# The last 512 rows of w_down on partitions 0 to 63, loaded in two pieces of 32 partitions

## The chip, the cores and the metric

The kernel runs on one core of one Trainium2 chip. The metric is the device time of one execution in microseconds (us). "The span" is what the profile shows, from the first to the last instruction; the time is about 2 us longer than the span. Before the change the median is 123.2 us.

## The reference, cut to what matters

```python
x  = A_x                                   # [8, 1, 512]
xn = layernorm(x)
s  = attention(xn, k_cache, v_cache, wq, wo)   # last 1024 keys, 32 heads on 8 kv heads
g  = silu((gelu(xn @ w_gate) * (xn @ w_up)) @ w_down)   # 512 -> 1792 -> 512
return x + s * g
```

Eight rows of activations meet 47.5 MB of weights and cache, each byte used once. So the kernel is a stream of loads with a little work behind it. In the order of loading: K, wq, then K and V in turn, w_gate, w_up, w_down (1792 rows of 512 numbers in bf16, 1 KB a row), and wo in four blocks of 1 MB.

## The kernel before

All loads of weights and cache go out from SyncE's queue, each a DMA of 128 partitions:

```python
    def load_ffn():
        ...                                    # w_gate, w_up: two loads of 896 KB each
        JH = JF // 2                           # JF = 14 rows of w_down per partition
        wd = B_w_down.rearrange("(p j) d -> p j d", j=JF)
        for a in range(2):
            t = slot()[:, 0 : JH * D].rearrange("p (j d) -> p j d", j=JH)
            nc.sync.dma_start(out=t, in_=wd[:, a * JH : (a + 1) * JH, :])
            wd_t.extend(t[:, j, :] for j in range(JH))
    ...
    def load_wo(m, cut=HS):                    # HS = 8; the last block in two pieces, 6 + 2
        t = slot().rearrange("p (e d) -> p e d", e=HS)
        src = A_wo[m * HS * Dh : (m + 1) * HS * Dh, :].rearrange("(p e) d -> p e d", e=HS)
        for lo, hi in ((0, cut), (cut, HS)):
            if lo < hi:
                nc.sync.dma_start(out=t[:, lo:hi, :], in_=src[:, lo:hi, :])
        wo_t[m] = t
```

The up and down projections run on TensorE in four groups of 32 columns (NQ = 4, Q = 32):

```python
    def ffn_up():                              # 2 x 4 x 4 matmuls of 512 columns
        ...
                cols = wt[k // 2][:, k % 2, :].rearrange("x (p j) -> x j p", j=JF)
                for q in range(NQ):
                    nc.tensor.matmul(gu_ps[w][Q * q : Q * (q + 1), :], xpT_sb[:, k, :],
                                     cols[:, j0[q] : j0[q] + JQ, :], ...)
    def ffn_down():                            # 14 x 4 matmuls
        ...
    # at the end: four output stores, two from SyncE's queue, two from ScalarE's
    for q in range(NQ):
        eng = nc.sync if q % 2 == 0 else nc.scalar
        eng.dma_start(out=out_flat[:, q * P : (q + 1) * P], in_=out_sb[32 * q : 32 * q + B, :])
```

The softmax here doesn't subtract the row's maximum and nothing guards it: scores larger than these inputs give would overflow.

## Time and profile before

| | before |
|---|---|
| time, median | 123.2 us |
| span | 121.1 us |
| chain of waits, share of DMA | 82% |
| 768 KB piece of the last A_wo block landed | 116.70 us |
| end of out_sb (last arithmetic) to end of span | 2.7 us |
| 16 KB packets of the instruction queue | 14 |

From the profile page of the kernel before: the span; then, in forty slices, the busy tenths of the sixteen DMA engines and their rate; then the instruction queue (packets, MB, share of time).

```profile
span 121.1 us, 4123 instructions
...
DMA  3999999999999999999999999999999999999820
GB/s 84 387 430 430 430 427 417 419 430 425 425 427 427 425 414 422 430 419 430 425 427 422 422 417 430 422 425 422 425 433 418 422 414 434 416 430 423 341 88 5
...
q8 instruction: 14, 0.23, 0.7%
```

The loads run at about 425 GB/s from the second slice to the 37th; the fall to 341 in slice 38 is the first sign that not all sixteen engines end together. The end of the chain of waits (start, length in us, what):

```profile
98.97 17.74 DMA slot<-in_A_wo_dram
116.70 0.04 issue
116.75 1.05 PE s_ps L383 x31
117.80 0.02 issue
117.82 0.30 DVE tmp L483
118.12 0.02 issue
118.14 0.29 DVE out_sb L485
```

A piece of A_wo lands, 1.05 us of matmuls follow, two VectorE steps, and the stores. From the timeline of the same kernel, the four blocks of that last projection (start, length, engine, line; in brackets the idle time before it and what ended it):

```profile
109.96 1.02 PE L383 MATMUL s_ps<-slot,oE_1066 128*8 128x128 bf16 x32 [0.32 <-DMA slot<-in_A_wo_dram]
112.40 1.02 PE L383 MATMUL s_ps<-slot,oE_1569 128*8 128x128 bf16 x32 [1.42 <-DMA slot<-in_A_wo_dram]
114.84 1.02 PE L383 MATMUL s_ps<-slot,oE_2072 128*8 128x128 bf16 x32 [1.42 <-DMA slot<-in_A_wo_dram]
116.75 1.02 PE L383 MATMUL s_ps<-slot,oE_2360 128*8 128x128 bf16 x32 [0.88 <-DMA slot<-in_A_wo_dram]
```

TensorE waits for every block. Work that is added ahead of it is free as long as it fits into these waits; work added to the loads is not.

One more reading is needed, which no view prints. A DMA of 128 partitions is sixteen shares, and each share raises the DMA's semaphore when it lands. The trace has these raises. Sorted, in us from the span's start, for the two pieces of the last A_wo block:

```
768 KB: 113.54 113.55 113.57 113.58 113.77 113.85 114.14 114.42 114.97 115.00 116.42 116.50 116.53 116.65 116.67 116.70
256 KB: 114.17 114.18 114.20 114.22 114.41 114.48 114.78 115.06 115.61 115.64 117.06 117.12 117.15 117.27 117.31 117.32
```

Sixteen equal shares end over 3.2 us. At 20 us they had lain within 0.3 us. The lag comes in steps of about 1.2 us, one beside each of the fourteen 16 KB packets of the instruction queue: by 74 us, after eight packets, eight engines are late by one step; the next six packets hit six of these a second time. These packets are refills of TensorE's instructions: it has 3714 instructions (1856 matmuls, 1856 weight loads and two semaphore waits), 14.5 times 256, and 256 instructions of 64 bytes make 16 KB. (That one is 64 bytes is this arithmetic.) A second instruction queue has 8 KB packets; the two that run beside loads (41.45 and 79.19 us) leave a smaller step, of 0.6 to 0.9 us, in one share each. A DMA is done when its last share is, so the kernel waits for the engines that carried most refills.

### The profile page before, as it was taken

To read this page: it belongs to the slowest core of one execution; us is meant where nothing else is said; L and a number is where in the kernel's file an instruction comes from. 1 tells how busy PE (TensorE), PEld (TensorE's weight loads), DVE (VectorE), ACT (ScalarE), POOL (GpSimd) and SP (SyncE) were. 2 spreads that over 40 slices of the span, in tenths; PEclk is the share of its full clock that TensorE was granted. 3 is DMA by queue.
4 is the path that set the end of the run, shared out by engine and by line. 5 is a ranking of instruction groups with operands and counts; after the bars stand their busy time and mean duration, and the time that the engine had idled before them with its cause. 6 is when DMAs were issued, how large, how long until landed. Compare 5 with 4: busy or idle time off the path is not lost.

```text
span 121.1 us, 4123 instructions
## 1 busy us (share of the span) xinstructions
PE 86.0 (71%) x1856; PEld 71.1 (59%) x1856; DVE 72.3 (60%) x150; ACT 22.6 (19%) x70; POOL 2.4 (2%) x15
## 2 busy tenths in 40 slices
PE   0075269696875968999997969566798789955450
PEld 0061029586865957999896969565698542134340
DVE  2352046866956749678989987747798670562000
ACT  0440000321303301212330330303033300300000
POOL 6100000000000000000000000000000000000000
PEclk9999756999999985559999999999999756995555
DMA  3999999999999999999999999999999999999820
GB/s 84 387 430 430 430 427 417 419 430 425 425 427 427 425 414 422 430 419 430 425 427 422 422 417 430 422 425 422 425 433 418 422 414 434 416 430 423 341 88 5
DMA packets 6929, 47.73 MB, mean 394 GB/s; under 512 B 888, under 2 KB 896, under 8 KB 1920
## 3 DMA queue, kind: packets, MB, share of 16 engines
q1 hardware_dynamic: 6800, 47.46, 93.7%
q8 instruction: 14, 0.23, 0.7%
q10 hardware_dynamic: 112, 0.02, 0.1%
q14 instruction: 3, 0.02, 0.1%
HBM read 47.46 MB, written 0.01 MB: 392 GB/s over the span
## 4 chain that ended last, share of the span: by engine, by line
DMA 82%; PE 12%; DVE 2%; SPq 1%; issue 0%
DMA slot<-in_A_k_cache_dram 44%; DMA slot<-in_B_w_gate_dram 16%; DMA slot<-in_A_wo_dram 15%; DMA slot<-in_A_wq_dram 7%; PE kT_ps L282 7%; PE m_ps L329 2%; PE sc_ps L294 2%; SPq L91 1%; PE s_ps L383 1%; DVE kT L286 1%; PE m_ps L316 1%; DVE sums L318 1%; SPq L103 0%; PE m_ps L370 0%; DVE tmp L483 0%
## 5 line engine op out<-in xcount | busy, mean ns | idle before, releaser
L286 DVE COPY kT<-kT_ps 128x1024 bf16<-128x1024 bf16 x64 | 42.2, 677 | 18.1 <-PE kT_ps L282 17.5
L282 PE MATMUL kT_ps<-ident,slot 128*128 128x128 bf16 x512 | 43.4, 234 | 9.9 <-DMA slot<-in_A_k_cache_dram 9.5
L282 PEld LDWEIGHTS <-slot 128*128 128x128 bf16 x512 | 32.6, 104 | 13.3 <-DMA slot<-in_A_k_cache_dram 10.1
L304 ACT ACTIVATE pT<-sc_ps,diag 128x128 bf16<-128x128 f32 x64 | 18.2, 368 | 70.6 <-PE sc_ps L294 70.6
L294 PE MATMUL sc_ps<-qT_all,kT 128*128 128x16 bf16 x512 | 22.9, 171 | 0.3 <-issue 0.3
L329 PE MATMUL m_ps<-pT,slot 128*128 128x16 bf16 x512 | 21.8, 170 | 1.2 <-issue 1.1
L329 PEld LDWEIGHTS <-slot 128*128 128x128 bf16 x512 | 18.6, 97 | 4.6 <-issue 3.1
L294 PEld LDWEIGHTS <-kT 128*128 128x128 bf16 x512 | 20.4, 99 | 0.0
L318 DVE TENSOR_REDUCE sums<-m_ps 128x16 f32<-128x512 f32 x16 | 10.9, 684 | 1.2 <-PE m_ps L316 1.2
L402 PE MATMUL m_ps<-slot,xpT_sb 128*32 128x512 bf16 x32 | 7.7, 1105 | 0.0
L316 PE MATMUL m_ps<-pT,ones_pp 128*128 128x512 bf16 x16 | 6.7, 416 | 0.7 <-ACT pT L304 0.7
L250 PE MATMUL m_ps<-slot,xnT_sb 128*32 128x512 bf16 x32 | 3.5, 527 | 4.2 <-DMA slot<-in_A_wq_dram 4.2
L234 PE MATMUL m_ps<-ident,xhat 8*128 8x8 bf16 x4 | 0.3, 168 | 7.0 <-DVE xhat L214 7.0
L259 DVE CAST q_sb<-m_ps 128x512 bf16<-128x512 f32 x2 | 1.3, 686 | 6.6 <-PE m_ps L250 6.6
L356 DVE TENSOR_TENSOR wide<-m_ps,hmask 64x1024 bf16<-64x1024 bf16 x4 | 4.9, 1216 | 0.5 <-PE m_ps L352 0.4
L483 DVE TENSOR_TENSOR tmp<-s_ps,g_sb 128x128 f32<-128x128 f32 x1 | 0.3, 292 | 7.1 <-PE s_ps L383 7.1
L250 PEld LDWEIGHTS <-xnT_sb 128*32 128x32 bf16 x32 | 0.8, 101 | 6.2 <-issue 5.8
L322 DVE RECIPROCAL recip<-sums 128x16 f32<-128x16 f32 x16 | 4.0, 253 | 0.6
L234 PEld LDWEIGHTS <-xhat 8*128 8x128 bf16 x4 | 0.2, 102 | 7.0 <-DVE xhat L214 7.0
L402 PEld LDWEIGHTS <-xpT_sb 128*32 128x32 bf16 x32 | 1.7, 117 | 4.3 <-issue 3.4
L338 DVE TENSOR_TENSOR oT_all<-m_ps,recip 128x16 bf16<-128x16 f32 x16 | 3.5, 218 | 0.4 <-PE m_ps L329 0.3
L352 PE MATMUL m_ps<-ident,oT_all 128*64 128x128 bf16 x4 | 1.0, 253 | 2.7 <-DVE sums L318 2.1
(71 smaller groups left out, 33.4 us busy)
## 6 DMA issues: line engine op xcount, KB each, us to landing
slot<-in_A_k_cache_dram SPq DMA_DIRECT2D x16, 1024.0 KB, 19.4
slot<-in_A_v_cache_dram SPq DMA_DIRECT2D x16, 1024.0 KB, 19.7
slot<-in_A_wq_dram SPq DMA_DIRECT2D x4, 1024.0 KB, 8.6
slot<-in_A_wo_dram SPq DMA_DIRECT2D x3, 1024.0 KB, 18.0
slot<-in_B_w_gate_dram SPq DMA_DIRECT2D x2, 896.0 KB, 20.0
slot<-in_B_w_up_dram SPq DMA_DIRECT2D x2, 896.0 KB, 18.9
slot<-in_B_w_down_dram SPq DMA_DIRECT2D x2, 896.0 KB
slot<-in_A_wo_dram SPq DMA_DIRECT2D x1, 768.0 KB, 17.7
```

The source lines that it names most:

```text
L250: nc.tensor.matmul(q_ps[n][Q * q : Q * (q + 1), :], xnT_sb[:, k, :], wq_t[k][:, hkv * NW : (hkv + 1) * NW], start=(k == 0), stop=(k == NDC ...
L282: nc.tensor.transpose(t_ps[:, c * P : (c + 1) * P], k_t[g][:, cc * Dh : (cc + 1) * Dh], ident)
L286: nc.vector.tensor_copy(out=kT[n], in_=t_ps)
L294: nc.tensor.matmul(sc[g][:, s * CB + c, :], kT[n][:, c * P : (c + 1) * P], qT_all[:, hkv, b0 : b0 + I, :], start=True, stop=True,)
L304: nc.scalar.activation(out=pT[g][:, :, i * rep : (i + 1) * rep], in_=sc[g][:, :, i * rep : (i + 1) * rep], func=ACT.Exp, bias=diag[:, i : ...
L316: nc.tensor.matmul(sums_ps, ones_pp, pT[g], start=True, stop=True)
L318: nc.vector.tensor_reduce(out=sums, in_=sums_ps.rearrange("p c m -> p m c"), axis=AX.X, op=ALU.add)
L322: nc.vector.reciprocal(out=recip[g], in_=sums)
L329: nc.tensor.matmul(oT[g], v_t[g][:, c * Dh : (c + 1) * Dh], pT[g][:, c, :], start=(c == 0), stop=(c == C - 1),)
L338: nc.vector.tensor_tensor(out=oT_all[:, hkv * rep : (hkv + 1) * rep, b0 : b0 + I].rearrange("p j i -> p i j"), in0=oT[g].rearrange("p (i j ...
L356: nc.vector.tensor_tensor(out=wide, in0=t_ps.rearrange("p (q e) -> p e q", e=HS) .unsqueeze(2) .to_broadcast([HS * B, HS, HS, DQ]), in1=hm ...
L402: nc.tensor.matmul(gu_ps[w][Q * q : Q * (q + 1), :], xpT_sb[:, k, :], cols[:, j0[q] : j0[q] + JQ, :], start=(k == 0), stop=(k == NDC - 1), ...
```

## The change

The intent: w_down need not be spread evenly. Its last 512 rows go to partitions 0 to 63 as eight rows each, in two pieces of 32 partitions. The DRAM side of each piece is written with an outer dimension of 8, so that the piece is cut in eight shares of four partitions, on DMA engines 0 to 7 (by the rule that the prediction cites; experiment e1 looks at it). These then carry 144 KB of w_down each, the others 80 KB, where all carried 112 KB. If the engines that are late are 8 to 15, this evens them out. The price is more and smaller instructions on TensorE, since the hidden dimension is now split 10 x 128 + 8 x 64. The code calls the rows on 128 partitions wide and those on 64 narrow.

```diff
-        JH = JF // 2
-        wd = B_w_down.rearrange("(p j) d -> p j d", j=JF)
+        JH = JW // 2                                   # JW = 10, F1 = 1280
+        wd = B_w_down[0:F1, :].rearrange("(p j) d -> p j d", j=JW)
         for a in range(2):
             ...
+        t = slot()[0:PN, 0 : JN * D]                   # PN = 64, JN = 8
+        wn = B_w_down[F1:F, :].rearrange("(y x j) d -> x y (j d)", x=NX, j=JN)
+        for h in range(2):
+            nc.sync.dma_start(out=t[32 * h : 32 * (h + 1), :], in_=wn[8 * h : 8 * (h + 1)])
+        wd_t.extend(t[:, j * D : (j + 1) * D] for j in range(JN))
 ...
-                for q in range(NQ):                    # up: one matmul of 512 columns
-                    nc.tensor.matmul(gu_ps[w][Q * q : Q * (q + 1), :], xpT_sb[:, k, :],
-                                     cols[:, j0[q] : j0[q] + JQ, :], ...)
+                for q in range(NQ):                    # up: one wide, one narrow, 448 columns
+                    for first, d, c in ((True, dst[:, 0:nw], wide_c[:, w0:w1, :]),
+                                        (False, dst[:, nw:FQ], narrow_c[:, n0:n1])):
+                        nc.tensor.matmul(d, xpT_sb[:, k, :], c, ...)
 ...
-        for c in range(JQ):                            # 4 transposes, 1 copy
+        for c in range(3): ...                         # 3 transposes of 128, 3 of 64, 2 copies
 ...
-        for j in range(JF):                            # down: 14 x 4 matmuls
+        for j in range(JW + JN):                       # down: 18 x 4, the last 8 x 4 with 64 rows
```

## The prediction

> **What bounds the kernel now.** The loads. The chain of waits is 82% DMA, and the slice table shows the sixteen DMA engines 90% or more busy at about 425 GB/s from slice 2 to slice 36. Its tail: the first piece (768 KB) of the last block of A_wo is landed at 116.70 us, then 32 matmuls of L383 (1.02 us), then two DVE steps and the output store. All other work ends in time: PE waits 1.4 us before each of the A_wo blocks 1 and 2 and 0.9 us before the last (timeline).
>
> **The loads are unequal.** The trace's semaphore records give the landing of each of a DMA's sixteen shares. At 20 us they lie within 0.3 us. For the 768 KB piece, eight shares land at 113.54 to 114.42 us, two at 114.97 and 115.00, six at 116.42 to 116.70. The last piece (256 KB): eight at 114.17 to 115.06, eight at 115.61 to 117.32. Between, steps of about 1.2 us appear, each beside one of the fourteen 16 KB packets of the instruction queue (22.5 to 113.7 us). The first eight packets delay eight different engines once, later ones six of these again. The Trainium skill (Runtime: NRT & Kernel Launch, "Instruction fetch mechanics") says that instructions are refilled in 16 KiB blocks by DMA; the trace agrees on the size. The records do not number the engines. Chaining packets by end and next start, the delayed engines of the first fetches are mostly ones that did not carry the 8-row x loads. The Trainium skill (DMA: Bandwidth & Descriptors, "Why a DMA increments its semaphore by 16 and not by 1") says a DMA of this kind uses the largest k up to 16 that divides the slowest dimension of both sides, on the lowest-numbered k engines. So x used engines 0 to 7, and the late half should be 8 to 15.
>
> **The change.** By the same rule each new piece (source outer dimension 8, destination 32) goes to engines 0 to 7. Of w_down an engine now moves 112 KB. After, engines 8 to 15 move 80 KB and 0 to 7 move 144 KB. An 8192-byte packet takes 306 ns from start to start, a 7168-byte one 268, a 6144-byte one 231; estimate for 5120 bytes 193. Late engines: 16 x 268 to 16 x 193, minus 1.2 us. Early engines: plus 8 x 306 minus 1.2, plus 1.25 us. The 768 KB piece then lands on the early half at 114.8 to 115.7, on the late half by 115.5; the last piece at 116.3. The tail starts 1.0 us earlier.
>
> **Added work, off the path.** 50 more matmuls with their weight loads: L402 grows from 32 to 64 shorter ones (448 columns per group instead of 512, narrow ones with a worse stride), the down projection from 56 to 72, transposes from 4 to 6; one more copy. Estimate: plus 0.5 to 2 us before A_wo's projection, which has over 2 us of slack. The extra instructions may bring one more fetch; it would fall on an engine delayed once only, so cost nothing. Two more DMAs and one more ring slot: issues run some 17 us ahead, no stall.
>
> **Prediction.** 122.2 us (minus 0.8%), 121.8 to 122.8. Faster by over 2%: 0.02; within 2%: 0.96; slower: 0.02.
>
> **What would show it.** The sixteen last shares land within about 2 us instead of 3.1, the last at 116.3; the wait of L383 for A_wo ends near 115.7; its 1.02 us is unchanged; span near 120.1.
>
> **What would make it wrong.** If the late half is 0 to 7: about 124.4. If the pieces spread over sixteen engines: no gain. If the narrow strided matmuls cost over 3 us more, PE becomes the end of the chain.

## The result, and the profile after

The changed kernel takes 125.11 us (median of 4 runs, 124.96 to 125.12) against 123.22 us: a ratio of 1.015, with a 95% interval of 1.0132 to 1.0167. It is 1.5% slower, clear of the noise though under 2%, where a gain of 0.8% was predicted; the measured time lies far outside the predicted range of 121.8 to 122.8 us.

From the page of the changed kernel:

```profile
span 123.4 us, 4227 instructions
...
DMA  3999999999999999999999999999999999999400
GB/s 72 406 420 433 425 425 428 428 430 425 422 425 420 422 417 425 420 428 420 433 420 425 425 430 425 422 420 425 425 418 430 417 425 421 429 428 393 164 5 5
...
q8 instruction: 14, 0.23, 0.7%
```

The full rate does not last longer, and the slack at the end has changed shape: one slice at 164 GB/s, where there had been one at 341. One engine seems to run on alone. The chain of waits ends so:

```profile
103.35 14.46 DMA slot<-in_A_wo_dram
117.81 0.04 issue
117.85 1.05 PE s_ps L399 x26
118.90 0.02 issue
118.92 0.30 DVE tmp L514
119.22 0.02 issue
119.25 0.29 DVE out_sb L516
```

The 768 KB piece lands at 117.81 us, 1.11 us later than before, where 115.7 was predicted. From there to the end of out_sb it is 1.73 us in both. The four blocks in the timeline:

```profile
109.67 1.03 PE L399 MATMUL s_ps<-slot,oE 128*8 128x128 bf16 x32
112.02 1.03 PE L399 MATMUL s_ps<-slot,oE 128*8 128x128 bf16 x32 [1.32 <-DMA slot<-in_A_wo_dram]
116.02 1.02 PE L399 MATMUL s_ps<-slot,oE 128*8 128x128 bf16 x32 [2.97 <-DMA slot<-in_A_wo_dram]
117.85 1.02 PE L399 MATMUL s_ps<-slot,oE 128*8 128x128 bf16 x32 [0.81 <-DMA slot<-in_A_wo_dram]
```

The first starts earlier than before, although TensorE had more to do before it, and the second too, by 0.4 us. Then the third block comes 4.0 us after the second instead of 2.44. The loss falls into one interval, between 112 and 116 us. The shares, from the semaphore records:

```
second block: 108.17 108.48 109.59 110.49 110.56 110.60 110.66 110.99 111.02 111.08 111.10 111.19 111.20 111.45 111.97 111.98
third block:  110.62 110.92 112.03 112.99 113.07 113.08 113.11 113.43 113.47 113.58 113.59 113.62 113.64 113.90 114.42 115.97
768 KB:       112.44 112.74 113.92 114.80 114.87 114.89 114.95 115.33 115.36 115.38 115.44 115.48 115.53 115.73 116.29 117.81
```

The plan has worked on fourteen engines: eleven of them are now within 1 us of each other, three are ahead. One of the two that were last at 111.98 needs 4.0 us for its 64 KB of the third block instead of 2.45, and is alone at the end by 1.5 us. The fourteenth 16 KB packet starts at 111.94 us. So it seems that the last engine was loaded by the change and then struck by a refill; if so, it is not one that the change relieved. Experiment e11 tests this.

The second loss is at the very end: from the end of out_sb (119.54) to the end of the span (123.4) it takes 3.9 us, before it took 2.7. SyncE's waits after 118 us, changed kernel (who waited for whom: us in total, times, longest):

```profile
SPq L519 <- DVE out_sb L516: 13.7, 1, 13.7
SPq L547 <- DMA out_dram<-out_sb: 1.6, 1, 1.6
```

and the kernel before:

```profile
SPq L488 <- DVE out_sb L485: 13.1, 1, 13.1
SPq L516 <- DMA out_dram<-out_sb: 0.7, 3, 0.4
```

One wait of 1.6 us for a store stands where there had been three short ones. The stores of the two kernels in the timeline, before and then changed (start, length, queue, count):

```profile
118.47 0.71 SPq L488 DMA_DIRECT2D out_dram<-out_sb  x2
118.47 0.65 ACTq L488 DMA_DIRECT2D out_dram<-out_sb  x2
```

```profile
119.56 1.07 SPq L519 DMA_DIRECT2D out_dram<-out_sb  x2
119.57 0.65 ACTq L519 DMA_DIRECT2D out_dram<-out_sb  x2
```

ScalarE's two stores go out in 0.65 us as before; SyncE's take 1.07 instead of 0.71. In the trace SyncE pauses 0.45 us before its second store, and the store's last share lands at 122.33 us, 0.74 us after its other shares; between, at 121.01 us, an 8 KB packet of the second instruction queue starts. So the longer end has three parts: the last store starts 0.37 us later after out_sb than before (the pause), takes 0.57 us longer to land (its one late share), and 0.22 us more pass from its landing to the end of the span. The last part goes with the order in which SyncE waits for the semaphores at the end, which e12 looks at.

In sum: +1.1 us by the loads and +1.2 us at the end make the span 2.3 us longer. The time rose by 1.9 us only. The part of the time outside the span was 2.1 us for the kernel before and 1.7 to 1.9 us for the changed one in the four runs; nothing in the profile explains that part, and it stays open.

### The profile page after: what moved, and what is told of

It reads as the page before. It is cut to its first block, busy times and chain, and to the rows that moved or that the text cites. A ratio compares the mean times of both kernels' runs of the same rounds, so it can differ in the third digit from the quotient of the medians.

```text
span 123.4 us, 4227 instructions
## 1 busy us (share of the span) xinstructions
PE 85.5 (69%) x1906; PEld 72.5 (59%) x1906; DVE 71.7 (58%) x151; ACT 22.5 (18%) x70; POOL 2.4 (2%) x15
## 4 chain that ended last, share of the span: by engine, by line
DMA 93%; SPq 2%; PE 1%; DVE 0%; issue 0%
DMA slot<-in_A_k_cache_dram 59%; DMA slot<-in_B_w_up_dram 15%; DMA slot<-in_A_wo_dram 12%; DMA slot<-in_A_wq_dram 7%; SPq L101 1%; PE s_ps L399 1%; SPq L113 0%; DVE tmp L514 0%; DVE out_sb L516 0%; SPq L149 0%; SPq L120 0%
## 5 line engine op out<-in xcount | busy, mean ns | idle before, releaser
L298 PE MATMUL kT_ps<-ident,slot 128*128 128x128 bf16 x512 | 42.6, 231 | 11.7 <-DMA slot<-in_A_k_cache_dram 11.3
L298 PEld LDWEIGHTS <-slot 128*128 128x128 bf16 x512 | 32.0, 103 | 15.6 <-DMA slot<-in_A_k_cache_dram 12.4
L345 PEld LDWEIGHTS <-slot 128*128 128x128 bf16 x512 | 18.4, 96 | 3.1 <-issue 1.3
L399 PE MATMUL s_ps<-slot,oE 128*8 128x128 bf16 x128 | 4.1, 306 | 5.1 <-DMA slot<-in_A_wo_dram 5.1
L424 PE MATMUL m_ps<-slot,xpT_sb 128*32 128x384 bf16 (+3 forms) x64 | 6.8, 589 | 0.0
L266 PE MATMUL m_ps<-slot,xnT_sb 128*32 128x512 bf16 x32 | 4.2, 618 | 3.7 <-DMA slot<-in_A_wq_dram 3.7
L399 PEld LDWEIGHTS <-oE 128*8 128x8 bf16 x128 | 3.2, 116 | 5.9 <-issue 5.9
L332 PE MATMUL m_ps<-pT,ones_pp 128*128 128x512 bf16 x16 | 6.0, 376 | 0.7 <-ACT pT L320 0.7
L424 PEld LDWEIGHTS <-xpT_sb 128*32 128x32 bf16 x64 | 3.3, 119 | 2.7 <-issue 2.5
```

The costliest lines, as they stand in the source:

```text
L266: nc.tensor.matmul(q_ps[n][Q * q : Q * (q + 1), :], xnT_sb[:, k, :], wq_t[k][:, hkv * NW : (hkv + 1) * NW], start=(k == 0), stop=(k == NDC ...
L298: nc.tensor.transpose(t_ps[:, c * P : (c + 1) * P], k_t[g][:, cc * Dh : (cc + 1) * Dh], ident)
L332: nc.tensor.matmul(sums_ps, ones_pp, pT[g], start=True, stop=True)
L345: nc.tensor.matmul(oT[g], v_t[g][:, c * Dh : (c + 1) * Dh], pT[g][:, c, :], start=(c == 0), stop=(c == C - 1),)
L399: nc.tensor.matmul(s_ps[32 * q : 32 * q + B, :], oE[m][:, e, :], wo_t[m][:, e, q * P : (q + 1) * P], start=(m == 0 and e == 0), stop=(m == ...
L424: nc.tensor.matmul(d, xpT_sb[:, k, :], c, start=(k == 0 and first), stop=(k == NDC - 1), skip_group_check=True,)
```

## The experiments

Theory A: the late engines are not 8 to 15; some are in 0 to 7, and the one struck by the fourteenth refill has got the extra load. Theory T: the end is longer because of SyncE's own instructions. Rivals: the added work of TensorE, the added DMAs as such, and the extra load on engines 0 to 7 alone, without refills.

### e1_map: which engine is late

```diff
+    def mark(k):                       # 128 bytes to each of k partitions: k shares
+        nc.sync.dma_start(out=mark_sb[0:k, k * 64 : (k + 1) * 64],
+                          in_=A_wq[0:k, k * 64 : (k + 1) * 64])
 # kernel before, with mark(15) ... mark(1) one by one behind the later big loads
```

> The kernel before with fifteen tiny marker loads of 1 to 15 partitions (128 bytes each) between the last big loads; results stay right. The landing of a marker of k partitions gives the lag of DMA engines 0 to k-1, so the markers number the engines. The step that I relied on (late half = engines 8 to 15) expects every engine of the 8-partition marker to be among the eight early ones (lag under 0.9 us), and all of 8 to 15 late by 1.2 us or more. Theory A (read off the landings of the changed kernel) expects six of the late eight above 7 and two of them in 0 to 7, and that one of these two is struck by the fourteenth instruction refill. Time as before within 0.5 us.

The run is a single one (state unknown, 123.64 us, 768 KB piece at 116.70 us, as in the kernel before). The landings of the markers of 9 to 5 partitions (k shares each; each marker also has one early raise by the sequencer itself, left out):

```
9: 89.23 89.27 89.33 89.34 89.43 89.90 90.13 90.69 90.73
8: 91.78 91.83 91.84 91.96 92.44 92.66 93.15 93.19
7: 93.92 93.95 94.08 94.52 94.75 95.32 95.37
6: 96.09 96.13 96.24 96.68 96.92 97.54
5: 98.26 98.31 98.40 98.82 99.09
```

Each marker is a list of lags of engines 0 to k-1. From 9 to 8 an early engine drops out: engine 8 is early. From 8 to 7 again: engine 7 is early. From 7 to 6 one of the two late ones goes, from 6 to 5 the other: engines 6 and 5 are late. Engines 0 to 4 are early. The markers of more partitions place engines 9, 10 and 11 among the late, and leave one early engine in 12 to 15 that they don't number. So the assumption that the late half is 8 to 15 is wrong in two places of eight, and theory A's first half is shown.

The page "DMA: Bandwidth & Descriptors" of the Trainium skill, section "Why a DMA increments its semaphore by 16 and not by 1", says that such a DMA uses the largest k up to 16 that divides the slowest dimension of both sides, on the lowest-numbered k engines. The trace agrees with the count: a marker of k partitions had k landings for each k from 1 to 13 that was read, and each 32-partition piece had 8. That they are the lowest-numbered engines is the page's word; the nesting of the lists above fits it.

### e11_map_after: which engine ends last in the changed kernel

```diff
 # changed kernel
         load_wo(m, cut=HS if m < NM - 1 else HS - 2)
+        if m == 2:
+            for k in (5, 6, 7, 8):
+                mark(k)
```

> The changed kernel with four marker loads of 5, 6, 7 and 8 partitions between the third and the last block of A_wo: their landings give the lags of engines 0 to 4, 0 to 5, 0 to 6 and 0 to 7 just there. Theory A expects that engine 5 or engine 6 is the one that lands last of all sixteen (1.5 us after the next) since the fourteenth refill struck it, so the marker of 5 partitions lands some 2 us before the third block's last share and the marker of 7 after it. If the last engine is above 7, all four markers land 1.5 us or more before it.

A single run (state unknown). The last share of the third block landed at 115.91 us, then came:

```
5: 113.22 113.33 113.81 113.90 114.13
6: 113.46 113.54 113.99 114.10 114.33 116.12
7: 113.72 113.76 114.17 114.30 114.52 114.60 116.33
```

The sixth engine, engine 5, is the last of all; engine 6 is next but one step better. Theory A's second half is shown: the change put 32 KB more on engine 5, and beside the fourteenth refill (112.18 us in this run) the same engine fell back by 1.5 us. One run shows which engine it is; that one share lands alone, 1.5 us after the rest and at 117.7 to 117.8 us, is the same in the traces of the changed kernel, e5 and e9. The time was 124.23 us, 0.9 us less than the changed kernel without markers, though the 768 KB piece landed at 117.77 us; the four more loads are SyncE's, and the end shrank from 3.9 to 3.0 us. That belongs to theory T below.

### e7_fewer: take the fourteenth refill away

```diff
     def transpose_block(n):            # changed kernel, wrong result on purpose
         g, s = n // NB, n % NB
+        if s == NB - 1:
+            kT[n] = kT[n - 1]
+            return
```

> The changed kernel, wrong results on purpose: the last of each group's four blocks of K is not transposed, the block before is used again. That takes 256 instructions from TensorE (3814 to 3558), one refill's worth, all else equal. Theory A (the fourteenth refill, at 111.9 us, strikes engine 5 or 6, which the change loaded more) expects thirteen refills before the loads end, the 768 KB piece of A_wo at about 116.3 us instead of 117.8, and about 123.6 us in all, the longer end kept. Rival (added load on engines 0 to 7 alone sets the end, refills or not): the piece stays near 117.8.

The last block of K in each group is replaced by the one before it, so the result is wrong on purpose, though the comparison with the reference still let it pass. The ratio to before was 1.0073 (1.001 to 1.0137; 123.65, 123.65, 123.75 and one 125.09 us, whose span was as short as the others'). Thirteen 16 KB packets came before the loads ended. The chain of waits:

```profile
103.24 13.09 DMA slot<-in_A_wo_dram
116.37 1.05 PE s_ps L402 x32
```

The 768 KB piece landed at 116.33 us, where theory A had 116.3 and the rival 117.8. The extra load on engines 0 to 7 is in this kernel in full, so by itself it costs nothing here (116.33 against 116.70 us before); with the refill on top it costs 1.5 us. The end is still 3.7 us long.

### e2_sixteen and e3_half: two controls that were none

```diff
-        for h in range(2):             # e2: same rows, same partitions, sixteen shares
-            nc.sync.dma_start(out=t[32 * h : 32 * (h + 1), :], in_=wn[8 * h : 8 * (h + 1)])
+        HC = JN * D // 2
+        for h in range(2):
+            nc.sync.dma_start(out=t[:, HC * h : HC * (h + 1)], in_=wn[:, :, HC * h : HC * (h + 1)])
```

> The changed kernel with its 64-partition piece of w_down loaded as two column halves of 64 partitions, source outer dimension 16: shares of four partitions on all sixteen engines. Everything else, TensorE work included, stays as changed. Theory A (the extra 1.25 us of load on an engine in 0 to 7 that is struck twice by refills) expects the 768 KB piece of A_wo to land about as before, near 116.7 us instead of 117.8. Rival B (the added instructions of TensorE, with the fourteenth refill at 111.9 instead of 113.7 us) expects it to stay near 117.8. The end of the program after out_sb took 2.7 us before and 3.9 us changed: if that goes with the engine assignment, the time is 123.2; if with the added instructions or loads, 124.3.

It ran 127.46 us, ratio 1.0354 (1.0314 to 1.0393): slower than everything else, which no theory had expected. The rate in stretches of 2 us (stretch, length, busy time of the engines, clock, DMA share, GB/s), e2_sixteen:

```profile
104.00:106.00 2.00, 1.57 (x16) 0.46 (x8) 1.22 (x4) 0.58 (x1) 0.00 (x0) 1.00 1.06 245
106.00:108.00 2.00, 0.91 (x14) 0.63 (x14) 1.25 (x5) 0.00 (x0) 0.00 (x0) 1.00 0.98 210
108.00:110.00 2.00, 0.92 (x48) 0.80 (x52) 0.15 (x1) 0.00 (x0) 0.00 (x0) 0.82 1.10 248
```

and the changed kernel in the first two of these:

```profile
104.00:106.00 2.00, 1.38 (x16) 0.47 (x8) 1.37 (x3) 0.46 (x1) 0.00 (x0) 1.00 1.06 445
106.00:108.00 2.00, 0.94 (x18) 0.66 (x22) 1.17 (x5) 0.00 (x0) 0.00 (x0) 1.00 0.99 418
```

While the narrow piece loads, all sixteen engines are as busy and move half as much. The page "SBUF — State Buffer" of the Trainium skill, section "Door 1: The DMA port swizzle", gives a reason: partitions 32 apart share one of sixteen ports, so partitions 0 to 63 reach eight ports only. Sixteen shares of four partitions put two engines on every port; the eight shares of the change put one. The trace agrees, with 210 to 248 GB/s instead of 418 to 445; no run here tells the port from another cause of the halved rate. So e2 is no test of theory A, and says that the eight-share form was the right way to fill 64 partitions.

> Half the dose: of the 64-partition piece, columns of the first half go to all sixteen engines, those of the second half in two pieces to engines 0 to 7. Theory A expects the latest landing half way between e2_sixteen and the changed kernel (about 117.2 us for the 768 KB piece), since one engine of 0 to 7 is last in both. Were the late engines all in 8 to 15, it would land earlier than in both, by about 0.6 us against e2_sixteen (about 116.1).

Its first column half is loaded with sixteen shares, the second in the two pieces of the change:

```diff
+        nc.sync.dma_start(out=t[:, 0:HC], in_=wn[:, :, 0:HC])
+        for h in range(2):
+            nc.sync.dma_start(out=t[32 * h : 32 * (h + 1), HC:], in_=wn[8 * h : 8 * (h + 1), :, HC:])
```

It ran 124.96 us (ratio 1.0145), with the 768 KB piece at 118.20 us, later than in the changed kernel. It has the same shared ports in its first half, so it is inconclusive about the dose.

### e4_four_loads and e6_five_loads: the end, in the kernel before

```diff
-            nc.sync.dma_start(out=t, in_=wd[:, a * JH : (a + 1) * JH, :])
+            for lo, hi in ((0, 3), (3, JH)):                                  # e4
+            for lo, hi in ((0, 3), (3, JH)) if a == 0 else ((0, 2), (2, 4), (4, JH)):  # e6
+                nc.sync.dma_start(out=t[:, lo:hi, :], in_=wd[:, a * JH + lo : a * JH + hi, :])
```

> The kernel before, w_down in four loads of 128 partitions instead of two: two more DMAs on the load queue, all engines equal, TensorE as before. If the longer end of the program (3.9 instead of 2.7 us after out_sb) comes from the two more DMAs and their semaphores, it shows here and the time is about 124.4; if from TensorE's instructions or the engine assignment, the time stays at 123.2.

123.48 us, ratio 1.0023 (1.0005 to 1.004), the end 2.9 us. Two more DMAs as such are not the cause.

> The kernel before with w_down in five loads of 128 partitions (e4_four_loads had four): one DMA more brings the second store to the 79th recorded instruction of SyncE. Nothing else of the change is in it. Theory T expects the end to grow from 2.9 (e4) to 3.9 us and the time from 123.5 to about 124.5. If T is wrong, the time is 123.6 as in e4.

124.50 us, ratio 1.0103 (1.0085 to 1.0122), the end 3.8 us. One load more than e4, and nothing of the change in it, costs 1.0 us. Its loads ended in time (768 KB piece at 116.94 us). SyncE's waits after 118 us:

```profile
SPq L519 <- DMA out_dram<-out_sb: 1.5, 1, 1.5
```

The list of SyncE's recorded instructions (counted from 0) tells the same in each kernel. Before number 79 there is a pause of 0.43 to 0.45 us in e4, e5, e6, e7, e2 and the changed kernel, and 0.6 to 0.8 us later an 8 KB packet of the second instruction queue starts. In the kernel before and in e4 number 79 comes after the stores: the pause falls into a wait and the packet starts after the last store has landed (120.35 against 120.29 us, and 120.59 against 120.45). In e6 and in the changed kernel number 79 is the second store.

### e5_one_store: take the store away from number 79

```diff
-        eng = nc.sync if q % 2 == 0 else nc.scalar       # changed kernel
+        eng = nc.sync if q == 0 else nc.scalar
```

> The changed kernel with three of the four output stores issued from ScalarE's queue and one from SyncE's (two and two before). In the changed kernel SyncE pauses 0.45 us before its 79th recorded instruction, which is its second store, and a refill of 8 KB of instructions runs beside that store (121.0 us); in the kernel before the 79th instruction comes after the stores. Theory T (the end is longer by 1.16 us because the second store stands at that instruction) expects the time from the end of out_sb to the end of the span to fall from 3.9 to about 3.1 us (one more store in sequence on ScalarE costs 0.34), and the time to fall from 125.1 to about 124.3. If the longer end belongs to the engine assignment or to TensorE's instructions, it stays at 3.9 us and the time at 125.1.

The expectation failed: 125.07 us (median; 125.06, 125.08, 125.19 and one of 124.16), the end 3.9 us in the profiled run. The pause of SyncE was there still, now without a store behind it. ScalarE's third store went out at 120.33 us, no later than the second one of SyncE had, but landed at 122.29 us all the same, with the 8 KB packet at 120.94 us beside it: six of its eight shares were there by 121.65 us, the last two came at 121.93 and 122.29. (A fifteenth 16 KB packet, at 118.68 us, is also in this run, and one share of each of the first two stores was late by 0.35 to 0.5 us.) So a pause before a store is not all of it, and theory T was mended: the refill that lands beside the stores costs too. How much belongs to each e5 does not tell, since its last store started as late as the paused one; the split above is from the changed kernel's own trace. The one run of 124.16 us, with a span 1 us shorter, has no trace.

### e9_after_five: let SyncE's refill come early

```diff
-            nc.sync.dma_start(out=t, in_=wd[:, a * JH : (a + 1) * JH, :])   # changed kernel
+            for lo, hi in ((0, 2), (2, JH)) if a == 0 else ((0, JH),):
+                nc.sync.dma_start(out=t[:, lo:hi, :], in_=wd[:, a * JH + lo : a * JH + hi, :])
```

> The changed kernel with w_down in five loads instead of four (its first 128-partition load is cut in two), so that SyncE's 79th recorded instruction is its first store, which SyncE reaches long before it may start, and the 8 KB refill that follows has time to land before the stores. Theory T, mended by e5 (not the pause of SyncE alone, but its refill landing beside the stores): the loads end as in the changed kernel (768 KB piece at 117.8 us), the end after out_sb falls from 3.9 to about 3.1 us as in e3, time about 124.3. If T is wrong it stays at 125.1.

124.41 us, ratio 1.0076 (1.0037 to 1.0114), the end 3.2 us. The 8 KB packet came at 109.26 us, and the 768 KB piece landed at 117.71 us, within 0.1 us of the changed kernel. Of the 0.5 us that the end still takes over the 2.7 of the kernel before, 0.3 is one late share of each store beside a fifteenth 16 KB packet (118.63 us), and 0.2 comes after the last landing. One more load makes the kernel faster, by making SyncE reach its number 79 while it has time. In e6, one more load had made the kernel before slower. Both follow from the place of SyncE's number 79, with its pause and its refill. (One of the four runs took 123.28 us with a span of 121.6; it has no trace, and its reason is open.)

### e8_four_engines, e10_four_again, e12_rotated: a version by the map

Engines 0 to 4 and 7 are early, 5 and 6 are not. Outer dimension 4 confines a piece to four engines (it had four landings), by the page cited under e1 to engines 0 to 3. The two pieces go to 16 partitions at 0 and 16 at 32; that this keeps an engine on one port is not tested here:

```diff
-    JW, JN, NX = 10, 8, 16                                 # against the changed kernel
+    JW, JN, NX, NY = 12, 8, 8, 4                           # 1536 rows wide, 256 narrow
 ...
+    wn_sb = persist.tile([PZ, JN * D], BF16, name="wn_sb")     # PZ = 48; rows 16 to 31 stay 0
+    nc.gpsimd.memset(wn_sb, 0.0)                               # paid with one ring buffer (21 -> 20)
 ...
         for h in range(2):
-            nc.sync.dma_start(out=t[32 * h : 32 * (h + 1), :], in_=wn[8 * h : 8 * (h + 1)])
+            nc.sync.dma_start(out=wn_sb[32 * h : 32 * h + 16, :], in_=wn[4 * h : 4 * (h + 1)])
 # down: 12 x 4 matmuls of 128 rows, 8 x 4 of 48 rows; w_down in five loads
```

The narrow rows have a buffer of their own, whose rows 16 to 31 are zero, so that one matmul of 48 rows can run over both pieces and never reads old data.

> A version meant to beat both: by the map of e1 engines 0 to 4 and 7 are early, 5 and 6 late. So 256 rows instead of 512 go to partitions 0 to 15 and 32 to 47, in two pieces whose source outer dimension is 4, so to engines 0 to 3 alone[...]; the other 1536 rows stay on 128 partitions. Engines 0 to 3 then move 160 KB of w_down, the others 96 instead of 112. Estimate from 306 ns per 8 KB packet: early ones plus 1.8, all others minus 0.6 us, so the 768 KB piece at 116.2 instead of 116.7 us. w_down comes in five loads so that the 79th instruction of SyncE comes before the stores. Time 122.7 to 123.1. If the map is wrong, the piece lands at 117 us or later.

e8 ran 123.02 us, ratio 0.9991 (0.9965 to 1.0017). The chain of waits ends with:

```profile
104.26 12.12 DMA slot<-in_A_wo_dram
116.38 0.04 issue
116.42 1.05 PE s_ps L405 x31
```

The piece landed at 116.38 us against 116.70 before. A loaded engine that was one step late would have ended near 116.8 us (115.0 before, and 1.8 more), so the map holds for engines 0 to 3, and the gain is 0.3 us of the 0.5 expected. The end took 3.0 us.

> The same kernel as e8_four_engines, timed more often: e8 had 122.91 to 123.10 us in its three timed runs and 123.51 in the profiled one, against 123.24 before. Expected 123.0, a ratio of 0.998, with an interval that shows whether it is under 1.

e10, the same kernel with more rounds, ran 123.09 us, ratio 0.9996 (0.9978 to 1.0015), so not shown to be faster. The gain in the loads (0.3 us) was given back at the end (3.0 instead of 2.7 us).

> e8_four_engines with A_wo in ten loads instead of five (halves of the first three blocks, quarters of the last). A reason for e8's longer end (3.0 us after out_sb against 2.7 before): at the end SyncE waits for the semaphores in a fixed order, and in e8 the last store is on one that is waited for first, so five more waits of 0.06 us each follow its landing; before, it was on the one waited for last. Five more loads rotate the stores back onto the last ones. Expected: loads end as in e8 (latest share of A_wo near 117.0), the end shortens by 0.3 us to 2.7, time 122.7, a ratio of 0.996 to before. If it is 123.0, the order of the waits does not matter.

```diff
-        for lo, hi in ((0, cut), (cut, HS)):
+        cuts = (0, 4, 8) if m < NM - 1 else (0, 2, 4, 6, 8)
+        for lo, hi in zip(cuts, cuts[1:]):
```

e12 ran 122.74 us (122.64 to 122.83), ratio 0.9968 (0.9954 to 0.9981). It beats the kernel before by 0.3%, clear of the noise, and so the changed kernel too, which was not timed in the same rounds. Its chain and SyncE's wait at the end:

```profile
117.20 0.04 issue
117.24 0.41 PE s_ps L405 x8
```

```profile
SPq L560 <- DMA out_dram<-out_sb: 0.9, 4, 0.4
```

The end is 2.7 us long, as expected, and the wait for the stores is four short ones again, not one of 1.1 us as in e8: the semaphores of the stores stand late in SyncE's fixed order, so each is passed while the next store is still landing. From the last landing to the end of the span it takes 0.84 us here and 1.15 us in e8. The 0.3% should not be read as the value of the load balance alone. The span is only some 0.15 us shorter than before (120.8 to 121.0 us in five runs against 120.9 to 121.2 in nine); the rest of the 0.42 us lies outside the span, where 1.8 us stand against 2.1, as in the changed kernel, for a reason that no run here shows.

## Why the prediction was wrong, point by point

The 2.9 us between 122.2 predicted and 125.1 measured are 2.1 us at the loads (the piece at 117.81 instead of 115.7 us) and 1.2 us at the end of the program, less 0.4 us outside the span.

**What bounds the kernel** was right: the loads, with the piece of A_wo at the end of the chain. TensorE's added work stayed off the path. The groups of the page, kernel before and then changed (line, engine, shapes, count, busy us, mean ns):

```profile
L402 PE MATMUL m_ps<-slot,xpT_sb 128*32 128x512 bf16 x32 | 7.7, 1105 | 0.0
```

```profile
L424 PE MATMUL m_ps<-slot,xpT_sb 128*32 128x384 bf16 (+3 forms) x64 | 6.8, 589 | 0.0
```

The up projection took 6.8 instead of 7.7 us although it has twice the matmuls, and A_wo's first block began at 109.67 instead of 109.96 us. Predicted was a cost of 0.5 to 2 us in the slack; there was none. A group has 448 columns instead of 512 now; but the granted clock in the two-microsecond stretches from 98 to 104 us was also higher (0.56, 0.59 and 1.00 against 0.50, 0.50 and 0.92), so how much belongs to the new form is not shown.

**That the loads are unequal, in steps of about 1.2 us, beside the refills** was right. e7 took one refill away and moved the end of the loads by 1.5 us.

**"So x used engines 0 to 7, and the late half should be 8 to 15."** This is the step that failed. The prediction's own evidence was weak: chains of packets, matched by end and next start, with ties, gave "mostly" engines without x loads for the first few refills, and I took that for all eight. e1 numbers the engines: 5 and 6 are late, 8 and one of 12 to 15 are early. The change put 1.25 us more onto engines 5 and 6, late by one step already, and in the changed kernel the fourteenth refill gave engine 5 its second step (e11). In the kernel before the fourteenth refill cost nothing: it struck one of the three engines that were one step late (113.1 to 113.3 us in the third block), and this one ended level with the five that had two (116.42 us against 116.50 to 116.70). Which engine it was no run numbers, nor what chose engine 5 in the changed kernel.

**The costs of the shares** were right. Early engines were to be 1.25 us later: the early eight ended at 113.5 to 114.4 us before, and the eleven in the middle of the changed kernel, which hold the loaded early ones, end at 114.8 to 115.7. The engines relieved were to end by 115.5: three stand ahead in the changed kernel, at 112.44, 112.74 and 113.92, where the earliest engine of before ended at 113.54. Had engine 5 not been struck, the piece would have landed at 116.33 (e7), against 115.7 predicted; the rest is that engines 5 and 6, loaded by the change, were one step late, where all loaded engines had been taken for early.

**"It would fall on an engine delayed once only, so cost nothing."** No refill was added while the loads ran: there were fourteen in the span in both. But the fourteenth fell on an engine that had been delayed once, was now loaded as well, and so had no room for it.

**"Two more DMAs ... no stall"** was right for the issue of the loads and missed the end of the program. More entries in SyncE's queue moved its number 79, with a pause and a refill, in among the stores, and the stores onto other semaphores: 1.2 us, more than half of what the span lost. e6 shows this without the change; in e9 and e11 most of it is gone from the changed kernel (ends of 3.2 and 3.0 instead of 3.9 us). The prediction named no such cost; among what could make it wrong it had the late half being 0 to 7 (124.4 us), which is nearer to the truth than the range it gave, in part by chance, since the end of the program is not in it.

## What to carry to other kernels

Before moving load between DMA engines, number them in the trace with marker loads of k partitions; a set inferred from a pattern is not a map, and one wrong engine of sixteen takes back the gain of all others. A balance within a microsecond also depends on where instruction refills fall: count the instructions of TensorE and of the queue that issues the stores, and look whether a refill lands in the last microseconds. A control that keeps the partitions but changes the number of shares may change the SBUF ports too.

## What the Trainium skill lacked or had wrong

- Runtime: NRT & Kernel Launch, "Instruction fetch mechanics": it calls the cost of crossing a 16 KiB boundary "mostly hidden". For the sequencer it may be; a DMA engine that is busy with loads lost about 1.2 us to each 16 KB packet, 1.5 us in one case (64 KB in 4.0 instead of 2.45 us), and the whole DMA waits for it. In e7, one refill fewer was worth 1.5 us. The page doesn't say which engines carry the refills; here eight of sixteen did in turn, 5, 6, 9, 10, 11 and three of 12 to 15.
- The same section gives blocks of 16 KiB. The second instruction queue's refills, of which the third moves with SyncE's count of instructions, were 8 KB each (8192 bytes), and one that came among the last stores cost 1.0 us, SyncE's pause before it included (e6 against e4).
- DMA: Bandwidth & Descriptors, "Latency and other measured facts": it says engines 7 and 15 are usually the slower ones, and ties this to another kind of descriptor generation than these loads use. So the runs do not contradict it, but for these loads it names no slow engine: here engine 7 was among the early ones, and 5 was the last (116.12 us in e11, where engines 0 to 4 were at 114.33 or before).
- DMA: Bandwidth & Descriptors, "Rules for kernel authors": it advises against two transfers to partition halves since both spread over all sixteen engines. Its row on using all sixteen has the exception that the change uses, a small outermost dimension, but as a loss only. Here it cost no rate: each piece had eight landings, and while they loaded the core moved 445 and 418 GB/s (104 to 108 us), since other engines went on with the next load (its first share landed at 105.69 us, the pieces' last at 107.08).
- No page has the order in which a program waits for its DMA semaphores at its end. The last store on the semaphore that was waited for first cost 0.3 us (e8's end of 3.0 us against 2.7 in e12).
